# The last stage's block sums move to GpSimd alone, with their DMAs, and leave the weights' conversion to VectorE and ScalarE

## Chip, cores and metric

The kernel runs on one core of one Trainium2 chip. The metric is the device time of one execution in microseconds (us); lower is better. Engines are named as in the profile: PE is TensorE, DVE is VectorE, ACT is ScalarE, POOL is GpSimd, SP is SyncE (here it only issues DMAs).

## What is computed

```
attn = block-causal attention, B=4, H=8, S=576, D=64, blocks of 64 positions
x    = attn as [4, 576, 512]
x    = sigmoid(xr @ w_r) * (relu(xk @ w_k)**2 @ w_v)   # xk, xr: mixes of x and the previous position
xn   = (x - mean) / sqrt(var + 1e-6) * g_ln            # the last stage begins here
out  = x + relu(xn @ w_ch1) @ w_ch2                    # w_ch1 [512, 2048], w_ch2 [2048, 512]
```

All arithmetic is of float32 accuracy: a matrix is held as two fp32r parts, high and low, and a product is three passes (high by high, low by high, high by low).

## The kernel before

Everything below is about the last stage, from about 465 us on. The 2304 rows of xn lie in five groups: 0, 1, 2, 3 of 512 rows and 4 (called Z) of 256. The 2048 columns of w_ch1 are taken in eight chunks c = 0 to 7 of 256; of each chunk, `em_c1` multiplies a group by the chunk's w_ch1 (24 matmuls of 512 columns, or of 256 for Z), ACT and DVE turn the sum in PSUM into relu's high and low parts (h1), and `em_c2` multiplies by the chunk's 256 rows of w_ch2 (6 matmuls for each 128 rows, 24 for a group of 512) and DVE adds the result to `acc` (L836). PSUM has five buffers `ph` for the first product and three `po` for the second. The em_c2 of one group is written behind the em_c1 of the next, so that PE has work while ACT and DVE make h1.

Two groups that form a pair can be done by a scheme with seven block products in place of eight (`em_c1s`, a Strassen-Winograd form): 42 matmuls for both groups where two em_c1 take 48. The pairs are P = (0, 3) and Q = (2, 1). The scheme needs four sums of blocks of the two groups' xn (tiles SF[0] to SF[3], 1 MB each, high and low parts) and four of the chunk's blocks of w_ch1 (tiles TF[c], called ta or tb). The sums of a pair don't change from chunk to chunk, but there is one set of SF tiles: the two pairs' sums are kept in DRAM (s_scr) and loaded by `load_form` (L754) while em_c1s goes on. Before the change P is done so from chunk 2 on, Q from chunk 4 on. The four sums are made once for each pair and each half k, by `sum_forms`: tensor_tensor operations (L695) on DVE, some on POOL, then `split`: ACT copies the high part, POOL subtracts for the low (L44). `dma_sums` (L751) then writes SF to s_scr or reads it back. P's sums are made during chunk 1, Q's half 0 during chunk 2 and half 1 during chunk 3.

At the same time the next chunk's weights are converted. They come as four pieces (loads L99 and L101, from SP, tile `raw`, two buffers); each goes through `above` and `below` (ACT, L41 a<-raw), `expo` (L130, here on POOL, since T["attention"] is set), `bits` (L134, DVE), `high` (ACT) and `low` (L44, POOL). `forms` (L605, DVE) makes the four sums of blocks of the weights in a third use of `raw`, and `t_high` (ACT) and `t_low` (POOL) split them into TF.

The order on each engine's queue is the order in which the program emits the instructions. Work beside the matmuls is emitted by `tick()`, which stands at some 17 places of a chunk: one tick emits one entry of `sums` (the block sums) and one of `turns` (a step of the conversion). All DMAs of this stage are issued from SP's queue.

Of the kernel before, what the change touches and what calls it, by code (L numbers as in the profile page):

```python
# [7 lines left out]
F32 = mybir.dt.float32  # L8
# [4 lines left out]
ALU = mybir.AluOpType  # L13
# [10 lines left out]
NC2 = DFF2 // CF  # L24
HORD = (3, 4, 5, 0, 1, 2)
GORD = (0, 3, 4, 2, 1)
PAIRS = ((0, 3), (2, 1))
# [5 lines left out]
def attention_moe_kernel(ctx, tc, raw_d, dup_d, raw0_d, dup0_d, v_d, v0_d, msk_d, mz_d, vec_d, eye_d, wk_d, wv_d, wr_d, wc1_d, wc2_d, out_d):  # L33
# [6 lines left out]
    def act(out, in_, func=AF.Copy, **kw):  # L40
        nc.scalar.activation(out=out, in_=in_, func=func, **kw)  # L41
# [545 lines left out]
    def chunk_jobs(c):  # L587
        L, kept = [], []
        for k in (0, 2):
            w = wc1_d[128 * k:128 * k + 256, CF * c:CF * c + CF].rearrange("(a p) n -> p a n", a=2)  # L590
            L.append(load_split(w, lambda i, k=k: W[c % 2][0][i][:, k:k + 2], kept))
        for k in range(2):
            r0 = CF * c + 128 * k
            L += pieces(wc2_d[r0:r0 + 128], lambda i: W[c % 2][1][i], k, DM)
        if c < 2:
            return L
        z = []

        def forms():
            (b11, b12), (b21, b22) = [[st["a2"].rearrange("p (a n) -> p a n", a=2)[:, :, o:o + 128] for o in (0, 128)] for st in kept]  # L600
            raw = stg2.tile([128, 4096], I8, name="raw8")
            z.append(raw.bitcast(F32).rearrange("p (i a n) -> p i a n", i=4, a=2))
            z1, z2, z3, z4 = [z[0][:, i] for i in range(4)]
            for out, in0, in1 in ((z1, b12, b11), (z3, b22, b12), (z2, b22, z1), (z4, b21, z2)):
                tt(out=out, in0=in0, in1=in1, op=ALU.subtract)  # L605

        load, above, below, expo, bits, high, low = [list(x) for x in zip(*[(l, a1, a2, x, b, h, w) for l, (a1, a2), (x, b), h, w in L])]
        t_high, t_low = lambda: act(TF[c][0], z[0]), lambda: sub(nc.gpsimd, TF[c][1], z[0], TF[c][0])
        return [
            [load[0], load[1]],  # L610
            [above[0], below[0]],
            [expo[0]],
            [bits[0], above[1], below[1]],
            [expo[1], high[0], load[2]],
            [bits[1], above[2], below[2], low[0]],
            [expo[2], high[1], load[3], low[1]],
            [bits[2], forms, above[3], below[3]],
            [expo[3], high[2], t_high],
            [bits[3], t_low],
            [high[3], low[2]],  # L620
            [low[3]],
        ]

# [61 lines left out]
    def sum_forms(pr, pool):  # L685

        (g0, g1) = pr
        v, g = nc.vector, nc.gpsimd
        st = {}

        def block(G, h, k):
            return [x[:, k].bitcast(F32) for x in quarter(G, h)]

        def op(eng, out, in0, in1, op=ALU.subtract):
            eng.tensor_tensor(out=out, in0=in0, in1=in1, op=op)  # L695

        def temp(n):
            st[n] = pool.tile([128, 512], F32, name="t")
            return st[n]

        def split(i, k, z):
            act(SF[i][:, 0, k], z)
            sub(g, SF[i][:, 1, k], z, SF[i][:, 0, k])

        def begin(n, a, b, how):
            op(g, temp("t" + n), a[1], b[1], how)
            op(v, temp("z" + n), a[0], b[0], how)

        def end(n):
            z = st["z" + n]  # L710
            op(v, z, z, st.pop("t" + n), ALU.add)
            return z

        def first(k):
            begin("1", block(g1, 0, k), block(g1, 1, k), ALU.add)

        def second(k):
            z = end("1")
            op(v, temp("y"), z, block(g0, 0, k)[0])
            split(0, k, st.pop("z1"))  # L720

        def third(k):
            op(v, st["y"], st["y"], block(g0, 0, k)[1])
            split(1, k, st["y"])

        def fourth(k):
            b = block(g0, 1, k)
            x = temp("x")
            op(v, x, b[0], st.pop("y"))
            op(v, x, x, b[1], ALU.add)  # L730
            split(3, k, st.pop("x"))

        def fifth(k):
            begin("3", block(g0, 0, k), block(g1, 0, k), ALU.subtract)

        def sixth(k):
            end("3")
            split(2, k, st.pop("z3"))

        def chain(k):  # L740
            return [lambda: first(k), lambda: second(k), lambda: third(k), lambda: fourth(k)]

        def other(k):
            return [lambda: fifth(k), lambda: sixth(k)]

        return chain, other

    def dma_sums(pr, out, k=slice(0, 2)):
        for i in range(4):
            m, s = s_scr[PAIRS.index(pr), i][:, :, k], SF[i][:, :, k].bitcast(F32)  # L750
            nc.sync.dma_start(out=m if out else s, in_=s if out else m)  # L751

    def load_form(pr, i):
        nc.sync.dma_start(out=SF[i].bitcast(F32), in_=s_scr[PAIRS.index(pr), i])  # L754

    def em_c1s(c, pr, nxt, prev, tick):

# [95 lines left out]
    with tc.manual_schedule():  # L853
# [299 lines left out]
                    ln_z(i, eng=nc.gpsimd if x == 2 else nc.vector)  # L1153

        Z = GORD[2]
        for x, G in enumerate(GORD):
            em_c1(0, G, lambda: norms(x))
            if x == 0:
                ln_scale(late[0], late[-1] + 1)
                conv = Convert(chunk_jobs(1))  # L1160
            cs = first[x]
            conv.some(cs[0])
            if x:
                em_c2(0, GORD[x - 1], (0, 1))
            conv.some(cs[1])
            if x:
                em_c2(0, GORD[x - 1], (2, 3))
            conv.some(cs[2])
        es_z.close()
        T["attention"] = True  # L1170
        todo = 0, GORD[-1]
        sums, turns = [], [[conv.step] for _ in range(2)]

        def open_sums(pr, *kk):
            es = ExitStack()
            chain, other = sum_forms(pr, opened(es, "tz", 4, side=R))

            def done(k):
                if pr == PAIRS[1]:
                    dma_sums(pr, True, k)  # L1180
                    dma_sums(PAIRS[0], False, k)

            for k in kk:
                sums.extend(other(k) + chain(k) if pr == PAIRS[0] else chain(k) + other(k))
                last = sums[-1]
                sums[-1] = lambda last=last, k=k: (last(), done(k))
            if pr == PAIRS[0]:
                sums.append(lambda: dma_sums(pr, True))
            sums.append(es.close)

        def open_forms(last, *cc):
            T["ef"] = es_f if last else ExitStack()
            ta = tf_tiles(opened(T["ef"], "ft", side=R), "ta")
            for c in cc:
                TF[c] = ta

        def close_forms(c):
            del TF[c]
            T["ef"].close()

        def tick():
            if sums:
                sums.pop(0)()
                if len(sums) == 1:
                    sums.pop(0)()
                    open_forms(*T["next"])
            if turns:
                for f in turns.pop(0):
                    f()
# [10 lines left out]
            return c, G  # L1220

        for c in range(1, NC2):
            P, Q = PAIRS
            if c == 1:
                T["next"] = False, 2
                open_sums(P, 0, 1)
                turns += [[], []]
            if c + 1 < NC2:
                turns += [[] for _ in range(5)] * (c in (2, 3)) + chunk_jobs(c + 1)
            if c == 1:  # L1230
                for G in (*P, Z, *Q):
                    todo = group(c, G, todo)
                continue
            one, two = (Q, P) if c in (5, 7) else (P, Q)
            em_c1s(c, one, two if c > 3 else None, [lambda ts=ts, x=todo: em_c2(*x, ts) for ts in ((0, 1), (2, 3))], tick)
            if c < 4:
                close_forms(c)
                T["next"] = (c == 3, 3) if c == 2 else (True, 4, 6)
                open_sums(Q, c - 2)
            tick()  # L1240
            todo = group(c, Z, (c, one[1]))
            if c < 4:
                for G in Q:
                    todo = group(c, G, todo)
            else:
                em_c1s(c, two, None, [lambda: em_c2(c, Z, (0, 1))], tick)
                todo = c, two[1]
                tick()
            if c == 3:
                del XN[g3, 0], T["o1"]  # L1250
                es_o.close()
                tb = tf_tiles(opened(es_f, "fb"), "tb")
                TF[5] = TF[7] = tb
        em_c2(*todo, range(4))


# [64 lines left out]
```

## Time and profile before

| | |
|---|---|
| time, median of 3 runs | 904.74 us (903.91 to 906.62) |
| the profiled execution: its own time, its span | 904.26 us, 902.5 us |
| busy in the span | PE 818.8 us (91%), DVE 567.8 (63%), ACT 421.7 (47%), POOL 350.2 (39%) |
| mean granted clock of TensorE | 0.97 of full speed |

"Busy" leaves out DMA issues and semaphore waits. The span runs from the first to the last instruction. A label such as `a<-raw` names the tile that is written and the tile that is read.

### The profile page before, as it was taken

To read this page: it belongs to the slowest core of one execution; us is meant where nothing else is said; L and a number is where in the kernel's file an instruction comes from. 1 tells how busy PE (TensorE), PEld (TensorE's weight loads), DVE (VectorE), ACT (ScalarE), POOL (GpSimd) and SP (SyncE) were. 2 spreads that over 40 slices of the span, in tenths; PEclk is the share of its full clock that TensorE was granted. 3 is DMA by queue.
4 is the path that set the end of the run, shared out by engine and by line. 5 is a ranking of instruction groups with operands and counts; after the bars stand their busy time and mean duration, and the time that the engine had idled before them with its cause. 6 is when DMAs were issued, how large, how long until landed. Compare 5 with 4: busy or idle time off the path is not lost. (4 is left out here: it accounts for less than half of the span.)

```text
span 902.5 us, 10604 instructions
## 1 busy us (share of the span) xinstructions
PE 818.8 (91%) x3768; PEld 672.1 (74%) x3768; DVE 567.8 (63%) x1000; ACT 421.7 (47%) x726; POOL 350.2 (39%) x283
## 2 busy tenths in 40 slices
PE   4988888999899999999999989985985898999998
PEld 4656765667689899899888778764774686877886
DVE  6898899887854424424775895653653564646544
ACT  6876877877663343445533333222322423424211
POOL 6799679756751101101212573242242321405000
PEclk9999999999999999999999999997996999999999
DMA  9995577415301010005250233052051607052243
GB/s 244 320 317 173 157 232 253 131 47 198 116 24 70 24 47 36 26 16 205 70 175 24 71 132 149 0 194 85 9 210 72 222 1 256 24 202 78 88 192 117
DMA packets 47301, 113.01 MB, mean 125 GB/s; under 512 B 4049, under 2 KB 18513, under 8 KB 44689
## 3 DMA queue, kind: packets, MB, share of 16 engines
q1 hardware_dynamic: 41776, 89.97, 29.1%
q0 software_dynamic: 5040, 20.01, 7.2%
q10 hardware_dynamic: 432, 2.36, 0.6%
q8 instruction: 30, 0.49, 0.2%
q14 instruction: 23, 0.18, 0.1%
HBM read 92.14 MB, written 20.19 MB: 124 GB/s over the span
## 5 line engine op out<-in xcount | busy, mean ns | idle before, releaser
L348 PE MATMUL po<-c,h 128*128 128x512 f32 x864 | 216.8, 403 | 35.0 <-DVE acc L836 34.4
L348 PEld LDWEIGHTS po<-c,h 128*128 128x128 f32 x864 | 165.7, 194 | 76.4 <-DVE acc L836 41.0
L348 PE MATMUL ph<-x,c 128*128 128x512 f32 (+1 forms) x528 | 112.5, 357 | 0.0
L836 DVE TENSOR_TENSOR acc<-po,acc 128x512 f32<-128x512 f32 x144 | 94.3, 684 | 23.2 <-PE po L348 22.4
L348 PE MATMUL s<-x,wk 128*128 128x384 f32 x576 | 103.1, 338 | 0.6 <-POOL x L44 0.3
L348 PEld LDWEIGHTS s<-x,wk 128*128 128x128 f32 x576 | 101.4, 188 | 2.1 <-POOL x L44 1.0
L348 PEld LDWEIGHTS ph<-x,c 128*128 128x128 f32 x528 | 89.1, 193 | 15.4
L348 PE MATMUL p<-wv,k 128*128 128x512 f32 x432 | 99.7, 390 | 0.6 <-DVE k L44 0.6
L44 POOL TENSOR_TENSOR x<-mix,x 128x384 fp32r<-128x384 f32 x36 | 40.4, 1136 | 152.5 <-ACT x L41 147.2
L41 ACT ACTIVATE a<-raw,ce 128x512 int32<-128x512 int8 (+1 forms) x80 | 57.3, 749 | 88.4 <-DVE a L134 45.6
L348 PE MATMUL p<-e,V 128*128 128x512 f32 (+4 forms) x320 | 96.7, 451 | 0.0
L348 PEld LDWEIGHTS p<-wv,k 128*128 128x128 f32 x432 | 80.9, 188 | 17.6 <-DVE k L44 1.0
L130 POOL TENSOR_TENSOR a<-a,a 128x512 int32<-128x512 int32 x32 | 43.9, 1371 | 126.7 <-ACT a L41 126.5
L348 PEld LDWEIGHTS p<-e,V 128*128 128x128 f32 x320 | 58.5, 197 | 34.8 <-issue 30.1
L44 DVE TENSOR_TENSOR k<-a,k 128x768 fp32r<-128x768 f32 x24 | 23.7, 988 | 81.5 <-ACT a L41 81.5
L134 DVE SCALAR_TENSOR_TENSOR a<-raw,a 128x512 int32<-128x512 int32 x52 | 59.5, 1144 | 19.3 <-POOL a L130 17.6
L44 POOL TENSOR_TENSOR c<-a,c 128x512 fp32r<-128x512 f32 x32 | 45.8, 1440 | 57.9 <-ACT c L41 57.9
L403 DVE TRANSPOSE_TENSOR_REDUCE part<-s 128x14 f32<-128x448 f32 (+4 forms) x160 | 65.1, 468 | 1.5 <-PE s L348 0.4
L348 PE MATMUL s<-wr,x 128*128 128x512 f32 x216 | 52.8, 405 | 3.1 <-DVE x L44 3.0
L41 ACT ACTIVATE u<-ph 128x512 f32<-128x512 f32 x30 | 17.9, 595 | 79.7 <-PE ph L348 74.4
L671 DVE SCALAR_TENSOR_TENSOR h<-ph,h 128x512 fp32r<-128x512 f32 (+1 forms) x40 | 23.2, 583 | 50.1 <-ACT h L41 50.1
L41 ACT ACTIVATE e<-s 128x1536 f32<-128x1536 f32 (+1 forms) x34 | 48.4, 1424 | 11.9 <-PE s L348 9.1
(155 smaller groups left out, 1225.9 us busy)
## 6 DMA issues: line engine op xcount, KB each, us to landing
s<-s_scr SPq DMA_DIRECT2D x16, 1024.0 KB, 6.9
kq<-in_dup_dram POOLq DMA_DIRECT2D x15, 1088.0 KB, 6.1
raw<-in_raw_dram SPq DMA_DIRECT2D x32, 288.0 KB, 4.6
raw<-in_w_ch_dram SPq DMA_DIRECT2D x16, 511.6 KB, 3.9
raw<-in_w_ch_dram SPq DMA_DIRECT2D x32, 255.6 KB, 4.8
V<-in_v_dram SPq DMA_DIRECT2D x16, 320.0 KB, 5.6
x_scr<-r SPq DMA_DIRECT2D x18, 256.0 KB, 2.0
acc<-x_scr SPq DMA_DIRECT2D x18, 256.0 KB, 4.8
```

The costliest lines, as they stand in the source:

```text
L41: nc.scalar.activation(out=out, in_=in_, func=func, **kw)
L44: eng.tensor_tensor(out=out, in0=in0, in1=in1.bitcast(F32), op=ALU.subtract)
L130: (nc.gpsimd if T.get("attention") else nc.vector).tensor_tensor(out=a1.bitcast(I32), in0=whole(a1), in1=whole(a2), op=ALU.subtract)
L134: stt(out=st["a2"].bitcast(I32), in0=w3, scalar=5, in1=st["a1"].bitcast(I32), op0=ALU.logical_shift_right, op1=ALU.bitwise_or)
L348: nc.tensor.matmul(out=out, lhsT=lhsT, rhs=rhs, start=start, stop=stop, **kw)
L403: red(out=pt[0:kp, b0:b0 + w // 32, j], in_=v3(s[0:kp, o:o + w]), axis=AX.X, op=ALU.max, apply_transpose=True)
L671: stt(out=h1[1][:, m, 0:n], in0=p[:, 0:n], scalar=0.0, in1=h1[0][:, m, 0:n].bitcast(F32), op0=ALU.max, op1=ALU.subtract)
L836: tt(out=acc[i], in0=p, in1=acc[i], op=ALU.add)
```

## The change

- `sum_forms` runs on POOL alone: every tensor_tensor, the copy of the high part (a tensor_scalar, formerly on ACT) and the subtraction. DVE and ACT have no part in it any more.
- `dma_sums` and `load_form` are issued from POOL's queue in place of SP's.
- POOL leaves the conversion: T["attention"] is no longer set to True in this stage, so `expo` runs on DVE; `low` (for chunks 2 to 7) and `t_low` run on DVE too.
- The conversion's steps stand in a new order of twelve entries (expo and bits of a piece in one entry).
- The work is placed anew: sum f3 of P's half 0 is emitted ahead of chunk 0's last group and half 1 behind it, the other six parts of P's sums in ticks 2 to 7 of chunk 1; group 3 goes ahead of group 0 in chunk 1. Q's sums are emitted in one piece behind em_c1s of chunk 2 (f3, both halves), 3 (f1, f2, f4 of half 0) and 4 (half 1), with their writes to s_scr and the reads of P's sums.
- The second pair joins the scheme from chunk 5 on (before: 4). In chunks 1 to 4 the conversion of the next chunk begins four ticks into the chunk.

```
         load, above, below, expo, bits, high, low = [list(x) for x in zip(*[(l, a1, a2, x, b, h, w) for l, (a1, a2), (x, b), h, w in L])]
-        t_high, t_low = lambda: act(TF[c][0], z[0]), lambda: sub(nc.gpsimd, TF[c][1], z[0], TF[c][0])
+        low = [lambda f=f: f(nc.vector) for f in low]
+        t_high, t_low = lambda: act(TF[c][0], z[0]), lambda: sub(nc.vector, TF[c][1], z[0], TF[c][0])
         return [
             [load[0], load[1]],
             [above[0], below[0]],
-            [expo[0]],
-            [bits[0], above[1], below[1]],
-            [expo[1], high[0], load[2]],
-            [bits[1], above[2], below[2], low[0]],
-            [expo[2], high[1], load[3], low[1]],
-            [bits[2], forms, above[3], below[3]],
-            [expo[3], high[2], t_high],
-            [bits[3], t_low],
-            [high[3], low[2]],
+            [expo[0], bits[0]],
+            [high[0], above[1], below[1], load[2]],
+            [expo[1], bits[1]],
+            [high[1], above[2], below[2], low[0], load[3]],
+            [expo[2], bits[2]],
+            [forms, above[3], below[3], high[2]],
+            [expo[3], bits[3], t_high],
+            [low[1], low[2]],
+            [high[3], t_low],
             [low[3]],
...
         def split(i, k, z):
-            act(SF[i][:, 0, k], z)
+            g.tensor_scalar(out=SF[i][:, 0, k], in0=z, scalar1=1.0, scalar2=0.0, op0=ALU.mult, op1=ALU.add)
             sub(g, SF[i][:, 1, k], z, SF[i][:, 0, k])
...
+        def both(a, b, how):
+            z, t = temp("z"), temp("t")
+            op(t, a[1], b[1], how)
+            op(z, a[0], b[0], how)
+            op(z, z, st.pop("t"), ALU.add)
+            return z
...
-            nc.sync.dma_start(out=m if out else s, in_=s if out else m)
+            nc.gpsimd.dma_start(out=m if out else s, in_=s if out else m)
...
-        nc.sync.dma_start(out=SF[i].bitcast(F32), in_=s_scr[PAIRS.index(pr), i])
+        nc.gpsimd.dma_start(out=SF[i].bitcast(F32), in_=s_scr[PAIRS.index(pr), i])
...
-        T["attention"] = True
+        f3(1)
...
+        turns = [[lambda: f1(0)], [lambda: f2(0)], [lambda: f4(0)], [lambda: f1(1)], [lambda: f2(1)], [lambda: f4(1)]]
+        turns += [[lambda: dma_sums(P, True, range(4))], [lambda: forms_for(2)]]
...
+        def sums_for(c):
+            del TF[c]
             T["ef"].close()
+            f1, f2, f3, f4 = open_sums(Q)
+            if c == 2:
+                for k in (0, 1):
+                    f3(k)
+            else:
+                for f in (f1, f2, f4):
+                    f(c - 3)
+            ii, k = ((2,), slice(0, 2)) if c == 2 else ((0, 1, 3), c - 3)
+            for pr, out in ((Q, True), (P, False)):
+                dma_sums(pr, out, ii, k)
+            forms_for(*((c + 1,) if c < 4 else (5, 7)))
```

The sums' temporaries (pool `tz`, four buffers) and the tiles TF (`ta`) lie in the same place, one after the other: `forms_for` closes the one and opens the other.

## Rows read from the trace of the kernel before

**Rows 1.** Busy time of each engine by chunk, chunks 1 to 7 (number of instructions in brackets).
```profile
500.80:556.54 55.74, 51.64 (x229) 42.11 (x228) 46.47 (x57) 21.03 (x35) 35.70 (x24) 0.97 0.37 137
556.54:622.74 66.20, 50.44 (x224) 40.64 (x223) 35.20 (x48) 18.04 (x30) 21.92 (x15) 0.92 0.27 95
622.74:689.14 66.40, 52.05 (x224) 41.95 (x223) 35.15 (x48) 18.07 (x30) 21.87 (x15) 0.89 0.22 80
689.14:742.31 53.17, 49.99 (x217) 40.63 (x216) 29.25 (x44) 17.77 (x29) 13.13 (x9) 0.95 0.33 119
742.31:794.41 52.10, 48.85 (x218) 39.87 (x216) 29.27 (x44) 17.76 (x29) 13.12 (x9) 0.97 0.34 122
794.41:845.96 51.55, 48.91 (x217) 39.90 (x216) 29.25 (x44) 17.75 (x29) 13.15 (x9) 0.97 0.33 123
845.96:902.50 56.54, 52.63 (x241) 43.11 (x239) 27.01 (x41) 9.35 (x16) 0.00 (x0) 1.00 0.42 158
```
**Rows 2.** Timeline of PE: start, length, instruction, idle time before it and releaser.
```profile
586.75 1.64 PE L348 MATMUL po<-c,h 128*128 128x512 f32 x6 [2.08 <-DVE acc L836]
...
620.01 2.93 PE L348 MATMUL po<-c,h 128*128 128x512 f32 x6 [12.22 <-DVE acc L836]
...
762.42 2.53 PE L348 MATMUL ph<-x,tb 128*128 128x512 f32 x6 [3.16 <-ACT u L41]
```
**Rows 3.** Timeline of ACT in chunk 2.
```profile
612.91 1.39 ACT L41 ACTIVATE a<-raw,ce 128x512 int32<-128x512 int8 x2 [13.83 <-DMA raw<-in_w_ch_dram]
```
**Rows 4.** Chain that ended last, in order of time: start, length, step.
```profile
604.83 7.99 DMA raw<-in_w_ch_dram
```
**Rows 5.** Timeline of SP's queue: chunk 2, then chunk 4.
```profile
586.59 14.06 SPq L751 DMA_DIRECT2D s_scr<-s  x4
600.70 4.08 SPq L751 DMA_DIRECT2D s<-s_scr  x4
604.83 0.63 SPq L101 DMA_DIRECT2D raw<-in_w_ch_dram  x1
...
694.47 1.71 SPq L754 DMA_DIRECT2D s<-s_scr  x2
696.24 1.84 SPq L99 DMA_DIRECT2D raw<-in_w_ch_dram  x4
```
**Rows 6.** POOL's operations by line: duration ns min/median/max, first and last start.
```profile
L138 POOL TENSOR_SCALAR wk<-a x4: 623/627/792, 211.6 to 223.9; 128x512 fp32r<-128x512 f32 x4
L695 POOL TENSOR_TENSOR t<-x,s x2: 1771/1772/1774, 505.8 to 523.2; 128x512 f32<-128x512 f32 x2
L44 POOL TENSOR_TENSOR s<-t,s x16: 1262/1296/1743, 511.4 to 664.5; 128x512 fp32r<-128x512 f32 x16
```
**Rows 7.** DVE's operations by line, the same columns.
```profile
L130 DVE TENSOR_TENSOR a<-a,a x8: 659/692/1810, 411.3 to 504.0; 128x512 int32<-128x512 f32 x8
L695 DVE TENSOR_TENSOR t<-t,x x12: 691/693/1811, 515.1 to 654.3; 128x512 f32<-128x512 f32 x12
L44 DVE TENSOR_TENSOR k<-a,k x24: 957/959/1362, 257.3 to 434.6; 128x768 fp32r<-128x768 f32 x24
L836 DVE TENSOR_TENSOR acc<-po,acc x144: 673/683/693, 465.7 to 898.7; 128x512 f32<-128x512 f32 x144
```
**Rows 8.** Timeline: POOL and DVE at the end of chunk 0.
```profile
500.69 1.31 POOL L44 TENSOR_TENSOR c<-a,c 128x512 fp32r<-128x512 f32 x1 [3.36 <-ACT c L41]
...
500.90 1.63 DVE L134 SCALAR_TENSOR_TENSOR a<-raw,a 128x512 int32<-128x512 int32 x1
...
504.58 1.30 POOL L44 TENSOR_TENSOR c<-a,c 128x512 fp32r<-128x512 f32 x1 [2.59 <-ACT c L41]
```
**Rows 9.** POOL's DMA issues by line (L242), then SP's of L751: duration ns, time to landing.
```profile
L242 POOL DMA_DIRECT2D kq<-in_dup_dram x15: 745/762/773, 8.1 to 161.5; - x15
DMA to landing us min/median/max: 5.3/6.1/9.5
...
DMA to landing us min/median/max: 3.1/5.6/7.3
```

More of the change, by code (lines that the diff above doesn't have):

```diff
@@ L687, in sum_forms @@
         (g0, g1) = pr
-        v, g = nc.vector, nc.gpsimd
+        g = nc.gpsimd
         st = {}
@@ L692, in block, with op @@
             return [x[:, k].bitcast(F32) for x in quarter(G, h)]
-        def op(eng, out, in0, in1, op=ALU.subtract):
-            eng.tensor_tensor(out=out, in0=in0, in1=in1, op=op)
+        def op(out, in0, in1, op=ALU.subtract):
+            g.tensor_tensor(out=out, in0=in0, in1=in1, op=op)
         def temp(n):
@@ L701, in split @@
         def split(i, k, z):
-            act(SF[i][:, 0, k], z)
+            g.tensor_scalar(out=SF[i][:, 0, k], in0=z, scalar1=1.0, scalar2=0.0, op0=ALU.mult, op1=ALU.add)
             sub(g, SF[i][:, 1, k], z, SF[i][:, 0, k])
[L705 to L711, printed above, removed]
-            return z
-        def first(k):
-            begin("1", block(g1, 0, k), block(g1, 1, k), ALU.add)
@@ L717, in second, with s1 @@
[L717 to L723, printed above, removed]
+        def both(a, b, how):
[3 more added lines that the diff above has]
+            op(z, z, st.pop("t"), ALU.add)
+            return z
+        def s1(k):
+            split(0, k, both(block(g1, 0, k), block(g1, 1, k), ALU.add))
@@ L724, in third, with s2, s4 @@
+        def s2(k):
+            a = block(g0, 0, k)
+            op(temp("y"), st.pop("z"), a[0])
+            op(st["y"], st["y"], a[1])
             split(1, k, st["y"])
-        def fourth(k):
+        def s4(k):
             b = block(g0, 1, k)
-            x = temp("x")
-            op(v, x, b[0], st.pop("y"))
-            op(v, x, x, b[1], ALU.add)
+            op(temp("x"), b[0], st.pop("y"))
+            op(st["x"], st["x"], b[1], ALU.add)
             split(3, k, st.pop("x"))
-        def fifth(k):
-            begin("3", block(g0, 0, k), block(g1, 0, k), ALU.subtract)
@@ L736, in sixth, with s3 @@
[L736 to L749, printed above, removed]
+        def s3(k):
+            both(block(g0, 0, k), block(g1, 0, k), ALU.subtract)
+            split(2, k, st.pop("z"))
@@ L750, in dma_sums @@
+        return [s1, s2, s3, s4]
+    def dma_sums(pr, out, ii, k=slice(0, 2)):
+        for i in ii:
             m, s = s_scr[PAIRS.index(pr), i][:, :, k], SF[i][:, :, k].bitcast(F32)
-            nc.sync.dma_start(out=m if out else s, in_=s if out else m)
+            nc.gpsimd.dma_start(out=m if out else s, in_=s if out else m)
     def load_form(pr, i):
-        nc.sync.dma_start(out=SF[i].bitcast(F32), in_=s_scr[PAIRS.index(pr), i])
+        nc.gpsimd.dma_start(out=SF[i].bitcast(F32), in_=s_scr[PAIRS.index(pr), i])
@@ L1155, in attention_moe_kernel, with open_sums @@
         Z = GORD[2]
+        P, Q = PAIRS
+        def open_sums(pr):
+            T["et"] = ExitStack()
+            return sum_forms(pr, opened(T["et"], "tz", 4, side=R))
         for x, G in enumerate(GORD):
@@ L1160, in attention_moe_kernel @@
                 conv = Convert(chunk_jobs(1))
+            if x == 4:
+                es_z.close()
+                f1, f2, f3, f4 = open_sums(P)
+                f3(0)
             cs = first[x]
@@ L1168, in attention_moe_kernel, with forms_for @@
             conv.some(cs[2])
-        es_z.close()
-        T["attention"] = True
+        f3(1)
         todo = 0, GORD[-1]
[L1172 to L1192, printed above, removed]
+        turns = [[lambda: f1(0)], [lambda: f2(0)], [lambda: f4(0)], [lambda: f1(1)], [lambda: f2(1)], [lambda: f4(1)]]
+        turns += [[lambda: dma_sums(P, True, range(4))], [lambda: forms_for(2)]]
+        def forms_for(*cc):
+            T["et"].close()
+            T["ef"] = ExitStack() if len(cc) == 1 else es_f
             ta = tf_tiles(opened(T["ef"], "ft", side=R), "ta")
@@ L1195, in open_forms @@
                 TF[c] = ta
-        def close_forms(c):
+        def sums_for(c):
             del TF[c]
             T["ef"].close()
-        def tick():
[L1202 to L1206, printed above, removed]
+            f1, f2, f3, f4 = open_sums(Q)
[9 more added lines that the diff above has]
+            forms_for(*((c + 1,) if c < 4 else (5, 7)))
+        def tick():
             if turns:
@@ L1222, in attention_moe_kernel @@
         for c in range(1, NC2):
-            P, Q = PAIRS
-            if c == 1:
[L1225 to L1231, printed above, removed]
+            if c + 1 < NC2:
+                more = chunk_jobs(c + 1)
+                if c == 1:
+                    turns[0:0] = [[conv.step], []]
+                    turns += [[] for _ in range(max(0, 16 - len(turns)))]
+                    for x, t in enumerate(more):
+                        turns[4 + x] = turns[4 + x] + t
+                else:
+                    turns += [[] for _ in range(4 * (c < 5))] + more
+            if c == 1:
+                for G in (P[1], P[0], Z, *Q):
                     todo = group(c, G, todo)
                 continue
[L1234 to L1239, printed above, removed]
+            one, two = (Q, P) if c == 6 else (P, Q)
+            em_c1s(c, one, two if c > 4 else None, [lambda ts=ts, x=todo: em_c2(*x, ts) for ts in ((0, 1), (2, 3))], tick)
+            if c < 5:
+                sums_for(c)
             tick()
             todo = group(c, Z, (c, one[1]))
-            if c < 4:
+            if c < 5:
                 for G in Q:
@@ L1248, in attention_moe_kernel @@
                 tick()
-            if c == 3:
+            if c == 4:
                 del XN[g3, 0], T["o1"]
                 es_o.close()
-                tb = tf_tiles(opened(es_f, "fb"), "tb")
-                TF[5] = TF[7] = tb
+                TF[6] = tf_tiles(opened(es_f, "fb"), "tb")
         em_c2(*todo, range(4))
```

## The prediction

> **What bounds the kernel now.** I read the busy time by chunk first, then the timelines of PE, ACT and SP around the longest gaps, then the prices of single operations. In chunk 7, where nothing is converted or summed, PE is busy 52.63 us at full clock with 228 matmuls of 512 columns (counting two of Z's 256-wide ones as one): 0.231 us each [rows 1]. At that pace chunk 1 (216 matmuls) would take 49.9 us, chunks 2 and 3 (210 each) 48.5, chunks 4 to 6 (204 each) 47.1. They take 55.74, 66.20, 66.40, 53.17, 52.10 and 51.55 [rows 1]. The excess over PE's pace is 5.9, 17.7, 17.9, 6.1, 5.0 and 4.5: 57.1 us in all. No engine is full in chunks 2 to 6 (DVE 35 of 66 us at most), so this excess is waiting, and part of it a granted clock of 0.89 to 0.97 behind the waits [rows 1].
>
> The longest gap shows what the waiting is. PE stands still for 12.22 us at 620.01, for DVE's addition to acc [rows 2]. DVE waits for relu from ACT, and ACT has stood for 13.83 us before an `above`, until a weight piece landed [rows 3]. That load was issued at 604.83 and took 7.99 us [rows 4]. It was late because of SP's queue: ahead of it stand four writes of sums, which took from 586.59 to 600.65 because each waits for POOL to finish a form, and then four reads that wait for the writes [rows 5]. So one queue in order makes the weights wait for the block sums. Chunk 3 has the same pattern. In chunks 4 to 6 it is milder: the first pieces' loads stand behind two `load_form`s that wait for PE (696.24 behind 694.47 [rows 5]), ACT stops before `above`, and PE stops for about 3 us for ACT's copy u (3.16 us at 762.42 in chunk 5 [rows 2]). A smaller gap, 2.08 us at 586.75 [rows 2], is DVE's queue standing behind a `bits` that waits for POOL's `expo`.
>
> **The change, part by part.**
>
> *SP's queue.* With dma_sums and load_form on POOL, only the weights' loads stay on SP, and a load waits for nothing but its raw buffer. The first two pieces of the next chunk can start as soon as bits[3] and t_low of the chunk before have read the old data, ahead of the chunk in which they are needed. The 13.83 us before ACT's `above` and its like in chunks 4 to 6 go. What is late next is DVE's own queue, below.
>
> *POOL's work.* Each pair and half takes 14 tensor_tensors and 4 tensor_scalars on POOL. I price the first at 1.30 us, the second at 0.63 [rows 6]: 20.7 us, four times 83 us. It loses 24 `expo`, 24 `low` and 6 `t_low`. When DVE works beside it a tensor_tensor takes up to 1.77 us, a tensor_scalar up to 0.79 [rows 6]; these are the upper bounds. In chunk 1, f3 of half 1 starts when POOL has finished a `low` of chunk 1's weights, which starts at 504.58 before [rows 8], so at about 505.9; to the end of f4 there are 25 tensor_tensors and 7 tensor_scalars, 36.9 us, to 542.8. Fifteen DVE operations fall beside them and each costs POOL the difference 1.74 - 1.30 = 0.45 [rows 6]: 549.5. By the upper bounds alone it is 555.7. PE needs the last form about 4 us into chunk 2, at 555 or later: covered at the value taken. In chunk 2, f3 twice (8 and 2) takes 11.7 us from the end of em_c1s, which is some 21 us into the chunk; in chunks 3 and 4 the 10 and 3 take 14.9, some 19 with DVE beside. So POOL ends near 40 us into a chunk of 50.
>
> *POOL's DMAs.* An issue on POOL took 0.76 us, 6.1 to landing [rows 9]. Three issues of writes, the first landing after about 5.6 [rows 9], and three of reads then come to 40 + 5.6 + 3 x 0.76 + 6.1 = 54 us; the next em_c1s needs the first form at 50 + 2.8 and the others 1.4 to 9 us later. I take 1 us for it in chunks 3 and 4, within the 2.5 below; the bounds are 0 and, with the longest landings of 7.3 and 9.5 [rows 9], 5 us each. Behind POOL's waits for a write, or in load_form for PE, only POOL's next DMAs are queued. In chunks 5 and 6 POOL's loads have half a chunk until the other pair is due.
>
> The Trainium skill (SBUF — State Buffer, SBUF: two separate sides) warns that a DMA issued on GpSimd stalls while VectorE runs an operation in a two-port mode, because its descriptors can't be written. The trace doesn't bear it out for this kernel's attention stage: 15 issues lie between 0.745 and 0.773 us [rows 9]. By that rule each of the six issues would take one VectorE operation longer, some 4 us in chunks 3 and 4, and the time would be about 866; by the row it is the sum below.
>
> *DVE's work.* It gets 24 `expo` and 24 `low` at 0.69, and 6 `t_low` of 1024 elements at 0.96 x 1024/768 = 1.28 [rows 7]: 41 us. It loses 32 sum operations at 0.69 [rows 7], 22 us and more, since several were stretched. Alone, that is at most +19 us over six chunks that leave DVE 9 to 31 us idle each [rows 1], which hides it. But a DVE operation with two SBUF operands doesn't run beside a POOL one: `bits` started at 500.90 inside a POOL operation and took 1.63 [rows 8], and the slowest took 1.81 against 0.69 [rows 7]; acc, with one operand in PSUM, never took over 0.693 [rows 7]. So where POOL runs without a break, a tick with expo and bits costs up to 3.5 us, not 1.4, and acc stands behind it. I followed the order of DVE's queue behind em_c1s: two such ticks (7.0), two of Z's relu (0.8), then acc: DVE gives back the first po buffer at 8.4 us, and PE, after Z (2.8) and three po tiles (4.1), wants it at 6.9. So PE loses 1.5 us there and some tenths later, and 1 for the forms: 2.5 us in each of chunks 2, 3 and 4. In chunk 1 POOL runs through, the ticks go on at 3.5 us, DVE is about 5 us behind at t_low, and t_low has also to wait until POOL has released the temporaries in whose place ta lies (549.5): 5 us, with 1 and 11 as bounds. Chunks 5 and 6 have no POOL operation beside DVE; 1 us each.
>
> *ACT* loses 16 copies. *The second pair's later start* costs 6 matmuls in chunk 4: 6 x 0.231 = 1.4 us, on PE's path.
>
> **Sum.** 57.1 - 1.4 - 5 - 3 x 2.5 - 2 x 1 = 41.2 us of gain. The profiled execution took 904.26, so 863.1; it lies 0.48 under the median, so 863.5 for the median, 863 in short.
>
> **The rivals.**
>
> *Almost no wait is left.* The chunks run at PE's pace. For it: chunk 7 does so with 27 us of DVE work [rows 1]. Against: POOL's runs stretch DVE. 904.7 - 57.1 + 1.4 = 849.
>
> *DVE becomes the bound in chunks 1 to 4.* For it: in chunk 1 DVE was busy 46.47 of 55.74 us already [rows 1]. [...] If each of the four loses 5 us more than I took, 883.
>
> *POOL is too slow, and the kernel slower than before.* ACT's t_high and DVE's t_low stand in their queues until POOL gives back tz, and the next em_c1s until the forms are there, so each us that POOL is late is one us of PE. There are 25 + 8 + 10 + 10 = 53 tensor_tensors in the four stretches. To eat the 41 us beyond the 3 or so of slack in each, they would have to be later by about 53 us, 1 us each: 2.3 us in place of 1.3. The slowest row is 1.77 [rows 6]. At 2.5 us it would be about 915.
>
> The Trainium skill (GPSIMD Engine Reference, Engine selection) puts two-input elementwise work on VectorE, with GpSimd about half as fast; the rows agree (1.30 and 0.69), and this rival is what that rule would lead to.
>
> *The change frees nothing.* If the raw buffers and not SP's queue held the load back, the gaps stay and 1.4 us come on top: 906. Against it: the load of 604.83 followed the reads ahead of it without a gap [rows 5].
>
> **How the numbers follow.** Chances: the forecast (850 to 877) 0.66, hardly a wait left 0.10, DVE the bound 0.18, POOL too slow 0.03, nothing freed 0.03. A difference of 0.3% (2.7 us) is about what a measurement of this kernel can tell. Faster 0.94; within it 0.02, half of the last case and a little; slower 0.04. The range 849 to 882 leaves out the two last cases, the upper half of DVE's, and what lies under PE's pace.
>
> **What would show it.** In SP's queue no load of weights behind a wait of some us; no ACT idle before a<-raw above 4 us; no gap of PE over 6 us in chunks 2 and 3, each about 51 us long; chunk 4 about 51, chunks 5 and 6 about 48; DVE's bits and expo at 1.6 or more beside POOL's runs and 0.69 in chunks 5 and 6; POOL's sums in unbroken runs of about 12, 19 and 19 us behind em_c1s. I am wrong if PE waits for ACT's ta or for the forms s, or if acc comes over 5 us late in each of chunks 1 to 4.

## The result, and the profile after

The changed kernel takes 871.92 us (median of 4 runs, 869.94 to 874.40) where the kernel before takes 905.38 (median of 4, 903.91 to 906.62): ratio 0.9632, 95% interval 0.9600 to 0.9665. The forecast was 863, range 849 to 882.

The busy time by chunk answers to [rows 1]; a chunk runs from its first matmul to that of the next. Columns: stretch, length, busy time of PE, PEld, DVE, ACT, POOL, granted clock, DMA share, GB/s.

```profile
502.14:559.87 57.73, 53.32 (x229) 42.82 (x228) 39.09 (x50) 16.16 (x27) 45.30 (x38) 0.94 0.32 114
559.87:612.73 52.86, 50.22 (x224) 41.01 (x222) 33.92 (x49) 15.79 (x26) 13.96 (x12) 0.97 0.28 100
612.73:665.13 52.40, 50.35 (x224) 40.99 (x223) 34.17 (x49) 15.82 (x26) 21.32 (x19) 0.97 0.30 101
665.13:715.86 50.73, 48.65 (x223) 39.88 (x222) 34.62 (x49) 15.93 (x26) 21.37 (x19) 1.00 0.30 103
715.86:765.09 49.23, 47.62 (x217) 38.64 (x216) 32.94 (x53) 17.82 (x29) 2.19 (x4) 1.00 0.36 129
765.09:814.11 49.02, 47.43 (x217) 38.69 (x216) 32.93 (x53) 17.80 (x29) 2.12 (x4) 1.00 0.29 108
814.11:871.40 57.29, 52.79 (x241) 43.12 (x239) 27.01 (x41) 9.36 (x16) 2.13 (x4) 1.00 0.41 156
```

Chunks 2 and 3 fell from 66.2 and 66.4 us to 52.9 and 52.4, chunks 4 to 6 by 2.4 to 2.9 each (chunk 4 in spite of six matmuls more), and chunk 1 grew by 2.0.

The gaps of PE that are left, on its timeline (answers to [rows 2]):

```profile
551.24 8.80 PE L348 MATMUL po<-c,h 128*128 128x512 f32 x23 [3.96 <-ACT h L41]
...
590.50 1.76 PE L348 MATMUL po<-c,h 128*128 128x512 f32 x6 [2.53 <-DVE acc L822]
592.06 7.15 PE L348 MATMUL ph<-x,c 128*128 128x512 f32 x24
...
642.80 2.69 PE L348 MATMUL po<-c,h 128*128 128x512 f32 x6 [1.97 <-DVE acc L822]
...
695.23 1.66 PE L348 MATMUL po<-c,h 128*128 128x512 f32 x6 [1.97 <-DVE acc L822]
...
745.64 1.66 PE L348 MATMUL po<-c,h 128*128 128x512 f32 x6 [1.53 <-DVE acc L822]
```

The gaps of 12 us are gone, and no gap is above 4 us. Three leave a mark beyond their length: 23 matmuls behind the first took 8.80 us where 5.3 is the pace, 24 behind the second 7.15 where 5.5 is, and six behind the gap of chunk 3 2.69 where 1.66 is usual. The granted clock, as a mean of its two levels of 2.4 and 1.2 GHz over the stretch, was 0.69 of full speed in 549 to 560 us, 0.77 in 592.0 to 599.2 and 0.56 in 642.8 to 645.4. The gap of chunk 4 is as long as that of chunk 3, 1.97 us, and the clock held behind it.

SP's queue in chunk 2 (answers to [rows 5]) holds nothing but weights, and POOL's in chunk 3 shows the sums as one run, then three writes, and three reads that wait for them:

```profile
583.97 6.26 SPq L101 DMA_DIRECT2D raw<-in_w_ch_dram  x2
602.56 5.55 SPq L99 DMA_DIRECT2D raw<-in_w_ch_dram  x4
```

```profile
631.26 2.60 POOL L696 TENSOR_TENSOR t<-o,x 128x512 f32<-128x512 f32 x2 [34.25 <-PE ph L348]
...
647.46 1.61 POOL L44 TENSOR_TENSOR s<-t,s 128x512 fp32r<-128x512 f32 x1
649.01 2.15 POOL L737 DMA_DIRECT2D s_scr<-s  x3
652.55 0.74 POOL L737 DMA_DIRECT2D s<-s_scr  x1 [1.39 <-DMA s_scr<-s]
```

The run takes 17.8 us and the waits for a write 0.7 to 1.4 us each (in chunk 2, where POOL has one write, 3.87); nothing of the conversion stands behind them. Of ACT's and DVE's queues two stretches matter. ACT in chunk 1:

```profile
549.64 1.06 ACT L41 ACTIVATE ta<-raw 128x1024 fp32r<-128x1024 f32 x1 [10.31 <-POOL s L44]
550.60 0.58 ACT L41 ACTIVATE h<-ph 128x512 fp32r<-128x512 f32 x1
```

and DVE in chunk 2, beside POOL's run:

```profile
586.51 1.66 DVE L130 TENSOR_TENSOR a<-a,a 128x512 int32<-128x512 f32 x1
588.20 1.64 DVE L134 SCALAR_TENSOR_TENSOR a<-raw,a 128x512 int32<-128x512 int32 x1
```

ACT's t_high waited 10.31 us for POOL's last subtraction, and relu stood behind it: that is the gap of 3.96. In chunk 2 expo and bits took 1.66 and 1.64 us, and acc stood behind them. With the pair before them (1.26 and 0.98 us, at 581.63) that is 5.5 us for four operations that take 2.8 with nothing beside them: the gap of 2.53.

### The profile page after: what moved, and what is told of

It reads as the page before. It is cut to its first block, busy times and chain, and to the rows that moved or that the text cites. A ratio compares the mean times of both kernels' runs of the same rounds, so it can differ in the third digit from the quotient of the medians.

```text
span 871.4 us, 10575 instructions
## 1 busy us (share of the span) xinstructions
PE 810.9 (93%) x3774; PEld 666.7 (77%) x3774; DVE 571.2 (66%) x1018; ACT 410.6 (47%) x707; POOL 345.3 (40%) x307
## 5 line engine op out<-in xcount | busy, mean ns | idle before, releaser
L348 PE MATMUL po<-c,h 128*128 128x512 f32 x864 | 214.2, 399 | 14.9 <-DVE acc L822 10.3
L348 PEld LDWEIGHTS po<-c,h 128*128 128x128 f32 x864 | 162.9, 191 | 56.7 <-DVE acc L822 17.8
L348 PE MATMUL ph<-x,c 128*128 128x512 f32 (+1 forms) x552 | 118.6, 358 | 0.0
L348 PEld LDWEIGHTS ph<-x,c 128*128 128x128 f32 x552 | 93.0, 191 | 16.0
L348 PEld LDWEIGHTS p<-e,V 128*128 128x128 f32 x320 | 57.7, 194 | 33.9 <-issue 29.0
L41 ACT ACTIVATE h<-ph 128x512 fp32r<-128x512 f32 (+1 forms) x53 | 27.8, 529 | 90.4 <-PE ph L348 90.4
L41 ACT ACTIVATE a<-raw,ce 128x512 f32<-128x512 int8 (+1 forms) x80 | 57.5, 750 | 26.0 <-DVE a L134 20.2
L41 ACT ACTIVATE u<-ph 128x512 f32<-128x512 f32 x27 | 16.1, 598 | 93.4 <-PE ph L348 92.0
L672 DVE SCALAR_TENSOR_TENSOR h<-ph,h 128x512 fp32r<-128x512 f32 (+1 forms) x44 | 26.0, 592 | 44.8 <-ACT h L41 44.7
L348 PE MATMUL s<-QK 128*128 128x512 f32 (+4 forms) x160 | 31.9, 331 | 21.5 <-DVE QK L436 21.2
L740 POOL DMA_DIRECT2D s<-s_scr x12 | 6.4, 537 | 113.9 <-PE ph L348 113.9
```

Source lines behind the costliest of these rows:

```text
L348: nc.tensor.matmul(out=out, lhsT=lhsT, rhs=rhs, start=start, stop=stop, **kw)
L672: stt(out=h1[1][:, m, 0:n], in0=p[:, 0:n], scalar=0.0, in1=h1[0][:, m, 0:n].bitcast(F32), op0=ALU.max, op1=ALU.subtract)
L740: nc.gpsimd.dma_start(out=SF[i].bitcast(F32), in_=s_scr[PAIRS.index(pr), i])
```

## The experiments

Length of each chunk in us, from the PE timelines, and the time of each run (medians; the ratio is to runs of the kernel before on the same chip).

| kernel | 1 | 2 | 3 | 4 | 5 | 6 | time | ratio, 95% interval |
|---|---|---|---|---|---|---|---|---|
| before | 55.7 | 66.2 | 66.4 | 53.2 | 52.1 | 51.6 | 905.4 | |
| changed | 57.7 | 52.9 | 52.4 | 50.7 | 49.2 | 49.0 | 871.9 | 0.963 (0.960 to 0.967) |
| queue alone | 54.2 | 64.5 | 64.5 | 47.1 | 47.2 | 47.2 | 887.5 | 0.979 (0.977 to 0.981) |
| split alone | 66.6 | 58.1 | 61.3 | 61.3 | 53.4 | 53.8 | 915.3 | 1.010 (1.008 to 1.012) |
| sums earlier | 51.0 | 52.8 | 50.9 | 50.7 | 49.2 | 49.0 | 866.0 | 0.955 (0.953 to 0.957) |
| no Q sums | 57.1 | 48.5 | 48.6 | 48.5 | 49.0 | 49.0 | 862.9 | 0.951 (0.949 to 0.954) |
| expo on POOL | 73.1 | 64.7 | 70.8 | 71.2 | 47.5 | 48.0 | 936.3 | 1.034 (1.030 to 1.038) |
| ta turned | 54.9 | 50.8 | 50.3 | 50.2 | 49.2 | 49.0 | 866.2 | 0.956 (0.953 to 0.959) |
| steps later | 57.5 | 52.9 | 52.4 | 50.7 | 49.0 | 48.9 | 873.2 | 0.964 (0.961 to 0.967) |
| steps sooner | 57.0 | 57.3 | 56.1 | 56.9 | 49.2 | 49.0 | 887.1 | 0.980 (0.977 to 0.983) |
| low back | 58.3 | 51.3 | 50.8 | 50.7 | 54.1 | 54.2 | 880.3 | 0.971 (0.968 to 0.973) |
| three together | 51.0 | 50.8 | 50.3 | 50.2 | 53.3 | 53.5 | 871.2 | 0.962 (0.958 to 0.965) |
| three, two later | 51.0 | 48.9 | 49.0 | 48.9 | 53.5 | 54.2 | 866.7 | 0.956 (0.953 to 0.959) |
| four together | 51.0 | 48.9 | 49.0 | 48.9 | 47.5 | 49.1 | 854.1 | 0.942 (0.941 to 0.944) |

### The two halves of the change, each alone

Queue alone: the kernel before, with

```
-            nc.sync.dma_start(out=m if out else s, in_=s if out else m)
+            nc.gpsimd.dma_start(out=m if out else s, in_=s if out else m)
...
-        nc.sync.dma_start(out=SF[i].bitcast(F32), in_=s_scr[PAIRS.index(pr), i])
+        nc.gpsimd.dma_start(out=SF[i].bitcast(F32), in_=s_scr[PAIRS.index(pr), i])
```

> The kernel before, with only dma_sums and load_form issued from POOL's queue in place of SP's. If SP's queue is what made the weights late: the 13.83 us wait of ACT for a raw piece is gone in chunks 2 and 3 and ACT's waits of 4 to 5 us in chunks 4 to 6 too; but POOL still has expo and low in its queue, and in chunks 2 and 3 it now stands until a write of sums has landed, some 5 to 8 us, so part comes back there: 875 to 890 us, chunks 4 to 6 at 48 to 50 us each. If the gain came from the new split of the work between the engines and not from the queue: 900 to 906 us.

Split alone: the changed kernel, with the same two lines turned back to nc.sync.

> The changed kernel, with dma_sums and load_form put back on SP's queue. If SP's queue is the cause: the loads of the third and fourth weight piece stand behind sums that POOL now makes in one run of 12 to 19 us, then behind the writes' landing; ACT waits 10 to 18 us for raw in each of chunks 2, 3 and 4 and some 4 us in chunks 5 and 6: 905 to 925 us, no better than before or worse. If the new split of the work is what gained: 870 to 880 us.

Measured: 887.5 and 915.3. Each half alone is worth -19.5 and +8.4 us against its own runs of before (906.95); both give -33.5. In the first, chunks 4 to 6 run at PE's pace (47.1), so there SP's queue was the whole excess. (Chunk 1 gains 1.5 us by the clock and not by the edit: see the last section.) But chunks 2 and 3 gain only 1.8 us each, less than I expected: the wait moved to POOL. POOL's timeline in chunk 2 of this kernel:

```profile
609.14 0.72 POOL L751 DMA_DIRECT2D s<-s_scr  x1 [1.66 <-DMA s_scr<-s]
609.88 1.27 POOL L130 TENSOR_TENSOR a<-a,a 128x512 int32<-128x512 int32 x1
```

and DVE's:

```profile
611.18 1.74 DVE L134 SCALAR_TENSOR_TENSOR a<-raw,a 128x512 int32<-128x512 int32 x1 [10.52 <-POOL a L130]
```

The last of eight DMAs goes out at 609.14, `expo` stands behind them, and DVE's bits waits 10.52 us for it, where ACT had waited 13.83 for a piece [rows 3]. In the split alone, SP and then ACT in chunk 2:

```profile
600.53 0.33 SPq L737 DMA_DIRECT2D s_scr<-s  x1
604.40 0.33 SPq L737 DMA_DIRECT2D s<-s_scr  x1
604.91 1.91 SPq L101 DMA_DIRECT2D raw<-in_w_ch_dram  x2
```

```profile
611.31 1.40 ACT L41 ACTIVATE a<-raw,ce 128x512 f32<-128x512 int8 x2 [12.00 <-DMA raw<-in_w_ch_dram]
```

Both weight loads go out behind the read of the sums, and ACT waits 12.00 us. In chunk 1 a load stands in the same way behind four writes of P's sums (539.05 to 549.00 us), and ACT waits 23.32. So the gain in chunks 2 and 3 needs both halves: whichever queue holds the sums' DMAs must hold no step of the conversion.

The Trainium skill (DMA: Bandwidth & Descriptors, Issuing engines are not separate DMA queues) says that issuing from several engines saves only the time of initiating a DMA, usually little. Here an issue took 0.33 us on SP and 0.7 to 0.8 at the median on POOL, and the move alone was worth 19.5: what it saved is the time for which the issuing queue waits, with what stands behind it. The measurement decides.

### POOL's expo put back

```
         todo = 0, GORD[-1]
+        T["attention"] = True
```

> The changed kernel, with expo of the weights of chunks 2 to 7 put back on POOL (T["attention"] set to True behind chunk 0, as before). If POOL's leaving the conversion is what lets Q's sums stand in one run: expo waits behind runs of 12 to 19 us and the landing of a write, bits on DVE waits for it with acc behind, and chunks 2, 3 and 4 take 8 to 18 us more each: 895 to 920 us. If one operation of four on POOL can be borne: within 5 us of 872.

Measured: 936.3, beyond the range expected. PE in chunk 3:

```profile
687.48 2.93 PE L348 MATMUL po<-c,h 128*128 128x512 f32 x6 [19.54 <-DVE acc L822]
```

and POOL:

```profile
658.36 2.62 POOL L696 TENSOR_TENSOR t<-o,x 128x512 f32<-128x512 f32 x2 [30.45 <-PE ph L348]
...
680.82 1.27 POOL L130 TENSOR_TENSOR a<-a,a 128x512 int32<-128x512 int32 x1
```

The first expo stands behind POOL's whole run with its DMAs, 22.4 us, and PE's gap is nearly as long. With expo alone on POOL, the sums in one run cost 64 us. In chunks 5 and 6, where POOL has no sums, the same edit makes them shorter (47.5 and 48.0 against 49.2 and 49.0): expo on DVE is what costs there.

### POOL's arithmetic beside DVE

No Q sums: `sums_for` without its calls of f1 to f4.

> The changed kernel, leaving out POOL's arithmetic for Q's sums in chunks 2, 3 and 4 (53 of its operations less 10 and 3 per call: 2 calls of f3, 2 each of f1, f2, f4); the DMAs stay, and Q's products in chunks 5 to 7 take other data. If POOL's operations beside DVE's with two SBUF operands make acc late: expo and bits take 0.69 us each there, PE's gaps of 2 to 2.5 us in chunks 2 to 4 shrink below 1 us, each of these chunks comes to 49 to 50 us, and the time falls by 4 to 8 us to 864 to 868. If DVE's queue alone makes them (chunks 5 and 6 have gaps of 1.5 us without POOL): the time falls by less than 3 us.

Measured: 862.9, 9.1 us less, somewhat more than expected. Chunks 2 to 4 of this kernel:

```profile
559.68:606.80 47.12, 47.01 (x218) 38.77 (x217) 29.89 (x48) 15.77 (x26) 2.67 (x4) 1.00 0.39 138
606.80:655.43 48.63, 48.55 (x224) 39.84 (x222) 30.57 (x49) 15.79 (x26) 4.29 (x6) 1.00 0.32 109
655.43:703.91 48.48, 48.37 (x224) 39.89 (x222) 30.56 (x49) 15.78 (x26) 2.15 (x3) 1.00 0.22 76
```

and DVE in its chunk 2, the same two operations as above:

```profile
584.09 0.68 DVE L130 TENSOR_TENSOR a<-a,a 128x512 int32<-128x512 f32 x1
584.81 0.69 DVE L134 SCALAR_TENSOR_TENSOR a<-raw,a 128x512 int32<-128x512 int32 x1
```

(The first of the three stretches begins 1.4 us into chunk 2.) PE is busy all but 0.1 us of each, at full clock, and DVE has 4 us less to do for the same operations. The three chunks are 10.4 us shorter together: 6.5 are the three gaps of the changed kernel, and some 3 the low clock behind two of them. The same gaps cost less in another execution: low back, below, has the same program in these chunks and gaps of 2.51, 1.96 and 1.96 us, the clock held, and the chunks took 51.3, 50.8 and 50.7, 7.2 above this kernel. So POOL's operations beside DVE's cost the three chunks 7 to 10 us, and without them DVE's longer list costs nothing. The sums' DMAs go out earlier here; that they cost nothing either is shown by the changed kernel, where PE never waited for a form s. The Trainium skill (SBUF — State Buffer, Who interferes with whom) says that a VectorE instruction with two SBUF inputs contends with a GpSimd one that reads SBUF, and that the lock on the ports that they share is exclusive. The rows agree, 1.64 us against 0.69 with nothing beside it.

Steps sooner: the conversion in chunks 2 to 4 begun at tick 0, only t_high and t_low kept at ticks 12 and 14.

```
...
-                    turns += [[] for _ in range(4 * (c < 5))] + more
+                    turns += more
```

> The changed kernel, with the conversion in chunks 2 to 4 begun at once in place of four ticks into the chunk, only t_high and t_low kept where they were (they need the place of the sums' temporaries). Expo and bits of the first two pieces then fall into em_c1s, ahead of POOL's run. If DVE's operations beside POOL's run make PE's gaps of 2 to 2.5 us: two of three contended ticks go, chunks 2 to 4 take 49.5 to 51 us each in place of 52.9, 52.4 and 50.7, the time is 866 to 869. If what DVE has to do in em_c1s is as tight: the gap comes back there, 871 to 874.

(The list with t_high and t_low in their new places is left out.) Measured: 887.1, a miss, by 15 us on the wrong side. DVE and PE in chunk 2 of this kernel:

```profile
584.23 1.18 DVE L605 TENSOR_TENSOR raw<-a 128x256 f32<-128x256 f32 x1
585.33 1.53 DVE L605 TENSOR_TENSOR raw<-a,a 128x256 f32<-128x256 f32 x1
586.79 2.93 DVE L605 TENSOR_TENSOR raw<-a,raw 128x256 f32<-128x256 f32 x2
...
589.97 0.76 DVE L130 TENSOR_TENSOR a<-a,a 128x512 int32<-128x512 f32 x1
590.76 1.63 DVE L134 SCALAR_TENSOR_TENSOR a<-raw,a 128x512 int32<-128x512 int32 x1
```

```profile
593.05 2.93 PE L348 MATMUL po<-c,h 128*128 128x512 f32 x6 [5.75 <-DVE acc L838]
```

Two pairs of expo and bits did leave POOL's run, but the other two came into it, and `forms` between them: four operations of 256 columns, 0.42 us each alone, took 5.6 us, 1.2 to 1.5 each, about as long as one of POOL's operations there (1.3 to 1.6 us). PE's gap grew to 5.75 us. So the number of DVE operations that fall beside POOL counted for more here than their length. The other direction is in "three, two later" below.

Steps later: four empty ticks ahead of the conversion in chunks 5 and 6 too (`range(4)` for `range(4 * (c < 5))`).

> The changed kernel, with the conversion in chunks 5 and 6 begun four ticks into the chunk as in chunks 2 to 4 (it was begun at once). PE has one gap of 1.5 us there in either chunk, before the fourth tile of the group ahead of Z, behind three conversion ticks of DVE. If the place of the steps makes it: the gap moves or goes, chunks 5 and 6 take 47.5 to 48.5 us and not 49.1, 870 to 871. If DVE simply has too much in these chunks (33 of 49 us busy): no change, or slower as the steps then fall beside the second em_c1s.

Measured: 873.2, no change; a gap of 1.1 us came behind the second em_c1s for one of 1.5 in Z. The gap did move, but the chunks (49.0 and 48.9) are no shorter, so the place of the steps alone is not what costs them.

### Chunk 1

Sums earlier:

```
                 f3(0)
+                f3(1)
             cs = first[x]
...
-        f3(1)
         todo = 0, GORD[-1]
```

> The changed kernel, with f3 of P's second half emitted right behind that of the first, ahead of chunk 0's last group. POOL stands idle there for 6.4 us. If chunk 1's 8 us over PE's pace come from t_high on ACT waiting for POOL's last sum (10.3 us): POOL's chain ends about 6 us earlier, the wait falls to about 4 us, PE's gap of 4 us and the low clock behind it go, chunk 1 takes 52 to 53.5 us and not 57.7, the time is about 867. If DVE's own queue is what makes chunk 1 late: the same time within 1.5 us.

Measured: 866.0. t_high's wait fell from 10.3 to 1.5 us, chunk 1 to 51.0, more than was expected. Chunk 3 is 1.5 us shorter too, which the edit doesn't touch: the gap of 1.98 us is there, and the clock held behind it.

ta turned:

```
-            ta = tf_tiles(opened(T["ef"], "ft", side=R), "ta")
+            ta = tf_tiles(opened(T["ef"], "ft", side=R), "ta")[::-1]
```

> The changed kernel, with the two tiles of ta taken in the other order, so that t_high writes the tile that lies where the other two temporaries lay. If each tile waits only for the temporaries in its own place: t_high waits for f2 and not for f4, ACT's wait of 10.3 us in chunk 1 falls to 2 us or less, t_low on DVE waits for f4 in its place; chunk 1 takes 53 to 56 us and not 57.7, the time is 867 to 870. If the place comes free only as a whole: no change, within 1.5 us of 872.

Measured: 866.2. So each tile waits only for what lay in its own place; but t_high still waited 6.20 us, for f4's first operation, which reads the temporary of f2. Chunk 1 lost 2.8 us. Chunk 2 lost 2.1 as well: PE's gap is shorter by half a us, and the clock holds behind it:

```profile
588.62 1.66 PE L348 MATMUL po<-c,h 128*128 128x512 f32 x6 [2.02 <-DVE acc L822]
590.12 5.60 PE L348 MATMUL ph<-x,c 128*128 128x512 f32 x24
```

24 matmuls take 5.60 us, not 7.15. The half us can be put down to the edit, the clock not: low back has the changed kernel's program in this chunk, and there the clock held behind the longer gap too:

```profile
591.21 1.66 PE L348 MATMUL po<-c,h 128*128 128x512 f32 x6 [2.51 <-DVE acc L823]
```

Against low back's chunks 2 to 4 this edit is worth 0.5 us each.

### Towards a better version

Low back:

```
-        low = [lambda f=f: f(nc.vector) for f in low]
-        t_high, t_low = lambda: act(TF[c][0], z[0]), lambda: sub(nc.vector, TF[c][1], z[0], TF[c][0])
+        e = nc.vector if c < 6 else nc.gpsimd
+        low = [lambda f=f: f(e) for f in low]
+        t_high, t_low = lambda: act(TF[c][0], z[0]), lambda: sub(e, TF[c][1], z[0], TF[c][0])
```

> The changed kernel, with low and t_low of the weights of chunks 6 and 7 (converted in chunks 5 and 6, where POOL has no sums) put back on POOL. If the work that DVE took over makes these two chunks 2 us longer than PE's pace (49.2 and 49.0 against 47.1): DVE has 4 us less in each, PE's gap of 1.5 us shrinks, 47.2 to 48.3 us each, the time falls by 1.5 to 3.5 us to about 869. If expo, bits and forms alone make the gap: within 1 us of 872.

Measured: 880.3, a miss: chunks 5 and 6 take 5 us more, not 1 to 2 less. POOL, DVE and PE in chunk 5 of this kernel:

```profile
741.75 2.78 POOL L44 TENSOR_TENSOR tb<-raw,tb 128x1024 fp32r<-128x1024 f32 x1
```

```profile
742.42 2.65 DVE L134 SCALAR_TENSOR_TENSOR a<-raw,a 128x512 int32<-128x512 int32 x1
```

```profile
745.73 2.93 PE L348 MATMUL po<-c,h 128*128 128x512 f32 x6 [4.14 <-DVE acc L823]
```

t_low is emitted in the same stretch as bits and holds DVE for 2.65 us; acc is late by more than before, and the clock goes down behind the gap of 4.14. Moving work off DVE helped (expo) or hurt (low, t_low) by what POOL's operation then lies beside.

Three together: sums earlier, ta turned and low back.

> The changed kernel with three edits: f3 of P's second half ahead of chunk 0's last group, ta's two tiles in the other order, low and t_low of the weights of chunks 6 and 7 on POOL. If each takes away its own wait: chunk 1 at 50.5 to 51.5 us, chunk 2 at 50.8, chunks 3 and 4 at 50.3, chunks 5 and 6 at 47.2 to 48.3: 856 to 860. If the first two take away the same wait: they give 6 us together and not 9, 862 to 865.

Measured: 871.2, beyond both ranges: chunks 1 to 4 as expected, 5 and 6 near those of low back, which had not been measured then.

Three, two later: the same, and six empty ticks in chunks 2 to 4.

> As the kernel with the three edits, and the conversion in chunks 2 to 4 begun six ticks into the chunk in place of four. Steps that fell beside POOL's run (it lasts 12 to 19 us from the end of em_c1s) come later: two of expo and bits pairs beside it instead of three. If DVE's operations beside POOL's are what is left in chunks 2 to 4: 0.5 to 1.5 us less in each, 1 to 4 us in all. If the last steps (t_low, the last low) come too late for the next chunk: PE waits for ta in em_c1s, 1 to 5 us more.

Measured: 866.7, 4.5 us less where 1 to 4 were expected; chunks 2 to 4 came to 48.9, 49.0 and 48.9, within 0.5 of PE's pace.

Four together: sums earlier, ta turned, six ticks, and `T["attention"] = c > 4` at the head of the loop over c, in place of low back.

> The changed kernel with the edits that the runs so far point to: f3 of P's second half ahead of chunk 0's last group, ta's two tiles in the other order, the conversion in chunks 2 to 4 begun six ticks into the chunk, and expo (not low) of the weights of chunks 6 and 7 on POOL, which has no sums there. By the chunks of the runs that had each edit: chunk 1 51.0, chunks 2 to 4 48.9 each, chunk 5 47.5, chunk 6 48.0 us, 293.2 in all where the changed kernel took 313.0: 850 to 856. If the edits stand in each other's way (a last step of a chunk too late for the next, expo on POOL late behind load_form): 858 or more, with a gap of PE in chunk 5.

Measured: 854.1 (853.06 to 856.35), ratio 0.942 to before. Its chunks 4 to 6:

```profile
652.20:701.08 48.88, 48.64 (x224) 39.88 (x222) 33.52 (x50) 15.81 (x26) 20.32 (x19) 1.00 0.32 108
701.08:748.55 47.47, 47.39 (x218) 38.72 (x216) 31.09 (x51) 17.84 (x29) 7.36 (x8) 1.00 0.41 145
748.55:797.60 49.05, 47.26 (x217) 38.77 (x216) 30.34 (x49) 17.85 (x29) 7.32 (x8) 1.00 0.30 108
```

The chunks add up to 294.3 us, 1.1 more than expected, all of it in chunk 6, which kept a gap of 1.7 us with expo off DVE. (The changed kernel's chunks add up to 312.0, not to the 313.0 of the expectation.) It beats the changed kernel by 18 us.

## Why the prediction was right, and where it was off

- **SP's queue as the cause: right, and shown** by the two halves. The forecast didn't say that the move of the DMAs alone would lose its gain in chunks 2 and 3; its words on what is queued behind POOL's waits held because POOL had left the conversion.
- **DVE's operations beside POOL's: right mechanism, too small.** I took 2.5 us for each of chunks 2 to 4, 1 of it for late forms; measured over PE's pace 4.4, 3.9 and 2.2 (52.86 - 48.5 and so on). Forms were never late. The gap that I had followed through DVE's queue at 1.5 us was 2.53, 1.97 and 1.97, and behind the first two the clock fell (0.97 in chunks 2 and 3), which the sum had not priced. In low back, where it held, the three chunks are 7.3 us over PE's pace, near the 7.5 taken: that total is right there by luck, as the us for forms made up for gaps taken too short.
- **Chunk 1: mis-sized, 5 taken, 7.8 measured.** The value for POOL's end was right (549.5 expected, 549.6 measured), in part by luck: the run began 1.3 us later and had one `low` more in it (1.31 us), and its operations took some 4 us more than their prices where 6.7 were taken. But I followed t_low on DVE and took t_high as free; the temporaries of the last sum lay in the place of t_high's tile, so ACT stood, with relu behind it. 3.96 us of gap and 3.5 of low clock follow. A wait of PE for ta was one of the signs named for being wrong; it came here, through ACT's queue, and in no other chunk.
- **Chunks 5 and 6: 1 us each taken, 2.1 and 1.9 measured.** "No POOL operation beside DVE" was right, and so was 0.69 for an operation; acc was late all the same, behind more of DVE's operations than before. With expo off DVE, chunk 5 came to 47.5; but chunk 6 kept a gap of 1.7 us in four together and none above 0.7 in POOL's expo put back, so the length of DVE's list is not all of it, and the rest stays open.
- **The matmuls of the later second pair: 1.4 us**, by count; no run has only that edit.
- **The sum.** The remainders come to 22.3 us where I took 14.5: 7.8 of the 10.0 us between the 863.1 forecast for a profiled execution and its 873.15. Chunk 1 also began 1.3 us later, and the last stretch is 0.75 longer.
- **The rivals.** "DVE the bound" set 5 us more than the forecast for each of chunks 1 to 4: chunks 2 and 3 took 1.9 and 1.4 more, chunk 4 none, and chunk 1's 2.8 came from t_high. "POOL too slow" came true at one place, t_high; its rule that each us of POOL's delay is one of PE's was too harsh there (10.31 us of ACT's wait gave a gap of 3.96). Its point of decision was never near: tensor_tensors ran at 1.3 to 1.9 us. "Nothing freed" is out.

## What to carry to other kernels

An in-order queue that waits for one thing delays everything behind it: before moving a DMA to another queue, list what stands behind its waits there; the move paid in full only with the conversion off POOL. Where two engines shut each other out by the instruction, count instructions that fall side by side, and move steps out of the other's run before shortening them. A tile that takes the place of another inherits its last reader: look at which one the first writer gets.

## What was not expected of the hardware

- Four 256-column operations on DVE took 5.6 us beside POOL's run and 1.7 alone.
- The clock did not go by the length of PE's gap. A gap of 2.53 us was followed by 24 matmuls at a granted clock of 0.77, one of 2.51 in low back by full clock; of two of 1.97 in the changed kernel one was followed by a fall. In chunk 1 the kernel before and queue alone have the same gap (the first line is of the kernel before):

```profile
534.25 2.93 PE L348 MATMUL po<-c,h 128*128 128x512 f32 x6 [3.41 <-DVE acc L836]
```

```profile
536.64 1.67 PE L348 MATMUL po<-c,h 128*128 128x512 f32 x6 [3.42 <-DVE acc L836]
```

  What decides it no run here shows, so a us or two of a chunk's length, where its clock differs, should not be put down to an edit.
- Three writes of 0.5 MB, issued on POOL one behind the other, cost it waits of only 0.7 to 1.4 us each, since they were under way together: the first read went out 3.5 us after the first write had begun to be issued (649.01 to 652.55), within the 3.1 to 7.3 of [rows 9].
